# Windows of 320 and 512 slots, an earlier first read of the slots, and scatters that follow evictions one by one

## The chip, the cores and the metric

The kernel runs on one NeuronCore of a Trainium2 chip. The metric is the device time of one launch in microseconds. The core has TensorE (PE in the profile, with its weight loads in a row PEld of their own), VectorE (DVE), ScalarE (ACT), GpSimd (POOL) and SyncE (SP), which issues the plain DMAs; POOL issues the indirect ones. PSUM is where PE writes; DVE and ACT copy it out ("evict").

## The reference

A gated linear attention with a complex decay feeds a mixture of experts with top 2 of 8:

```python
# attention: q, k, v, a_re, a_im are (4, 8, 768, 48): batch, heads, time, dim
scale = np.minimum(mag, 0.999) / (mag + 1e-06)          # mag = |a|
for t in range(S):
    S_re, S_im = ar * S_re - ai * S_im + kv(t), ar * S_im + ai * S_re
    y[:, :, t] = einsum('bhd,bhde->bhe', q[:, :, t], S_re)
# experts: x is y as (3072, 384); 8 experts, 384 -> 1024 -> 384
noisy_logits = x @ w_gate + log1p(exp(x @ w_noise)) * noise
top2, top2_w = ...                                       # softmax over the two largest
for e in range(E):
    for k in range(2):
        mask = top2[:, k] == e
        h = np.maximum(x[mask] @ w1[e], 0.0)
        out[mask] += top2_w[mask, k, None] * (h @ w2[e])
```

## The kernel before

**Attention.** Time is cut into 6 chunks of 128 steps; a chunk of the 4 batch rows is a *group* g of 4 tiles, 24 tiles n in all (n = 4g + b). The decay is put in polar form: phase p1 and p2 work out log magnitude and angle for a pair of tiles, p2t sums the angles along time with a matmul by a triangle of ones. The last row of each tile's angles is carried into the same batch row's next tile: a small DMA stores it in `car`, and `p2carry` adds it. Before the change `car` is the first partition of the tile `xga`. Per tile, `tr_unit(n, 0)` and `tr_unit(n, 1)` transpose the turned q and k on PE, and ACT evicts them (L302: first qT, then kT); `sc_unit` makes the scores (L310), `st_unit` the state update (16 small matmuls into pG, at partitions 0 and 64 for real and imaginary part, L320), `y_unit` the output into pY (L357 from the state, L359 from the scores), which ACT copies into xT (L360). `x_unit` turns it back into rows of the tile `xr` (one per group, two buffers).

**Routing.** After each group `glog` and `gdis` work out the gates. `gate_dispatch` gives every token two slots in the DRAM tensor `xs`: expert e owns a region of its own, rows are handed out in order of arrival, and a row holds the token's 384 values, its 8 gate weights and its number. POOL writes them with indirect DMAs ("scatters", L421), 8 per group: 4 tiles times 2 choices, 128 rows of 1600 bytes each. Groups 4 and 5 are dispatched in two steps, of three tiles and one. Scatters of groups 0 to 2 with b > 0 also wait for the copy L360 (`YC`) of tile 4(g + 1) + b - 1.

**Experts.** Each expert takes up to CAP = 832 slots in two windows: window 0 holds slots 0 to 383, window 1 slots 384 to 831. `load_x(e, w, dst)` reads a window from `xs` into `xga` (window 0) or `xgb` (window 1); `x_T` transposes it and splits it in two rounded parts; `mm1` multiplies with w1 (L544: 8 blocks of 128 hidden units, 9 matmuls each: 3 slices of the inner dimension, times high by high, high by low, low by high), ACT and DVE evict with relu and split; `mm2` multiplies with w2 per tile of 128 slots (24 matmuls of 384 columns, L568), the seventh tile being a half one of 64 (16 matmuls, L573 and L576). The result is multiplied with the gate, added to rows of `out` that `gather_o` (L555) has fetched, and scattered back (L582).

**Order.** The order on every engine is fixed at build time: each piece is given a step (`at(step, f, ...)`, step n being about tile n), the pieces are written out in order of steps, and a scheduler places them by readiness, priority and its own estimates of durations. At run time an engine takes its instructions in that order, so one that waits holds all behind it. Experts 0 and 1 are woven into the attention's end: `load_x(0, 0, xga)` stands behind the scatters of group 3, `x_T(0, 0)` at step 19, `load_x(1, 0, xga)` right behind it, then `mm1(0, 0)`, and `x_T(1, 0)` at step 23.3. The scatters of one launch are declared free of each other in `xs`; a read of `xs` waits for all scatters written before it, and later scatters wait for that read. In `out` each scatter waits for the one before it. At the end counts are checked: if an expert has more than CAP or fewer than 640 tokens, or experts 0 or 1 have less than a window 0 of them when it is read, a flag sends the launch down a slow path that is not run with these inputs.

Of the kernel before, what the change touches and what calls it, by code (L numbers as in the profile page):

```python
# [9 lines left out]
F32 = mybir.dt.float32  # L10
# [5 lines left out]
OP = mybir.AluOpType  # L16
# [61 lines left out]
def kernel(  # L78
# [20 lines left out]
    FILL = 640  # L99
    NQ = 2  # L100
    RAW = 3
    WIN = ((0, 384), (384, CAP - 384))
    JS = ((0, 1, 2), (3, 4, 5, 6))

# [43 lines left out]
    nc.gpsimd.memset(none[:, RNO:RNO + 1], float(NONE))  # L150
    xga = cp.tile([128, 4, ROW], F32, name="xga")
    nc.gpsimd.memset(xga, 0.0)
    car = xga[0:1, :, 0:HD]
    ncnt = cp.tile([128, 2], F32, name="ncnt")
    zero = cp.tile([128, DM], F32, name="zero")
    nc.vector.memset(zero, 0.0)
    ones_f = cp.tile([128, 1], F32, name="ones_f")
    nc.vector.memset(ones_f, 1.0)
    bad = cp.tile([128, 2, NT], F32, name="bad")
# [81 lines left out]

    def p2carry(m):
        if m >= B // 2:
            th = T0[m][2][0:1]
            b = 2 * m % B
            nc.vector.scalar_tensor_tensor(th, car[:, b:b + 2], -2.0 * math.pi, th, op0=OP.mult, op1=OP.add)

    def p2t(n):
        b, g = bt(n)
        pt = psC.tile([128, 512], F32, name="cum")  # L250
        nc.tensor.matmul(pt[:, :HD], tri_t, T0[n // 2][2][:, b % 2, :], start=True, stop=True)
        if n % 2 == 0:
            TF[n // 2] = pf.tile([128, 2, 2, HD], F32, name="tf", bufs=2)
        tf = TF[n // 2][:, :, n % 2, :]
        if g:
            nc.scalar.activation(tf[:, 1, :], pt[:, :HD], AF.Identity, bias=b_rnd)
            nc.vector.scalar_tensor_tensor(tf[:, 0, :], tf[:, 1, :], -RND, pt[:, :HD], op0=OP.add, op1=OP.subtract)
        else:
            nc.vector.tensor_scalar(tf[:, 1, :], pt[:, :HD], RND, -RND, op0=OP.add, op1=OP.add)
            nc.vector.tensor_sub(tf[:, 0, :], tf[:, 1, :], pt[:, :HD])  # L260
        if g + 1 < NG:
            nc.sync.dma_start(car[:, b, :], tf[127:128, 0, :])

    def p2s(m):

# [29 lines left out]
    def tr_unit(n, i):  # L295
        x = (qh, kh)[i][n % NQ]
        store = (QT, KT)[i]
        store[n] = pa.tile([112, H, 128], F32, name=("qT", "kT")[i], bufs=2)
        p = psA.tile([128, H, 128], F32, name="ptr", bufs=1)[0:112]
        for h in range(H):  # L300
            nc.tensor.transpose(p[:, h, :], x[:, h, :, :].rearrange("p r x -> p (r x)")[:, 0:112], ident)  # L301
        nc.scalar.activation(store[n], p, AF.Copy)  # L302

    def sc_unit(n, half):
        if half == 0:
# [7 lines left out]
    def st_unit(n):  # L313
        b, g = bt(n)
        if g + 1 == NG:
            return
        x = kh[n % NQ]
        for r in range(2):
            for h in range(H):
                nc.tensor.matmul(pG[64 * r:64 * r + D, h, :], x[:, h, r, 0:D], V[n][:, h, :], start=True, stop=True)  # L320

    def st_upd(n):
# [20 lines left out]
    def y_unit(n):  # L343

        b, g = bt(n)
        if b == 0:
            XR[g] = pa.tile([128, B, ROW], F32, name="xr", bufs=2)
            nc.gpsimd.memset(XR[g][:, :, RNO + 1:ROW], 0.0)
            nc.gpsimd.tensor_copy(XR[g][:, :, RNO], tokid[:, g])
        XT[n] = pa.tile([128, H // 2, 128], F32, name="xT", bufs=6)  # L350
        for i in range(H // 2):
            for z in range(0 if g else 1, 2):
                for r in range(2):
                    h = 2 * i + r
                    o = pY[64 * r:64 * r + D, i, :]
                    if z == 0:
                        nc.tensor.matmul(o, Z[b][:, h, :], QT[n][:, h, :], start=True, stop=False, skip_group_check=True)  # L357
                    else:
                        nc.tensor.matmul(o, V[n][:, h, :], AM[n][:, h, :], start=not g, stop=True, skip_group_check=True)  # L359
        LAST['y'] = YC[n] = nc.scalar.activation(XT[n], pY, AF.Copy)  # L360
# [28 lines left out]
            nc.tensor.transpose(p[:, kk * 128:(kk + 1) * 128], xt[:, b, kk * 128:(kk + 1) * 128], ident)  # L389
        return p  # L390

    scat, behind, YC = [], [], {}

    def gate_dispatch(g, lo, hi, lz):
        n = hi - lo
# [13 lines left out]
        nc.vector.tensor_add(pos, p[:, :n * E].rearrange("p (b e) -> p b e", b=n),  # L409
                             base_run[:, None, :].to_broadcast([128, n, E]))  # L410
        nc.vector.tensor_add(base_run, base_run, p[:, n * E:(n + 1) * E])
        if g == NG - 3:
            nc.vector.tensor_copy(ncnt, base_run[:, 0:2])
        nc.vector.tensor_mul(oh, oh, pos[:, None].to_broadcast([128, 2, n, E]))
        sl = pa.tile([128, 2, n], U32, name=f"sl{n}", bufs=2)
# [3 lines left out]
        for b in range(n):  # L419
            for kk in range(2):  # L420
                d = nc.gpsimd.indirect_dma_start(  # L421
                    out=xs, out_offset=bass.IndirectOffsetOnAxis(ap=sl[:, kk, b:b + 1], axis=0),
                    in_=XR[g][:, lo + b, :], in_offset=None, bounds_check=E * N - 1, oob_is_err=False)
                for s in scat:
                    tc.declare_no_dep(d.ins, s.ins, reason="slots differ")
                scat.append(d)

                if g < NG - 3 and b:
                    behind.append((d, B * (g + 1) + b - 1))


    fill = {}
# [11 lines left out]


    x3 = xs.rearrange("(e i) r -> e i r", e=E)
    TW = [min(128, CAP - 128 * j) for j in range(7)]

    def load_x(e, w, dst):
        if w == 0:  # L450
            nc.sync.dma_start(dst[:, 0:3], x3[e, 0:384].rearrange("(p j) r -> p j r", j=3))
        else:
            nc.sync.dma_start(dst[:, 0:3], x3[e, 384:768].rearrange("(p j) r -> p j r", j=3))
            nc.sync.dma_start(dst[0:CAP - 768, 3], x3[e, 768:CAP])

    mctx = ctx.enter_context(ExitStack())
    mpools, psB = [], []  # L460
# [49 lines left out]
    def x_T(e, w):  # L510
# [11 lines left out]
        for kk in range(KD):  # L522
            x = XW[w, kk] = mt([128, 2, n], F32R, name=f"x{w}{kk}")
            p = ps_tile("px")
            for j in js:
                o = 128 * (j - js[0])
                gz = nc.tensor.transpose(p[:, o:o + TW[j]], src_t[0:TW[j], j - js[0], kk * 128:(kk + 1) * 128],  # L527
                                    ident[0:TW[j], 0:TW[j]])
                if (e, w) == (0, 1):
                    behind_of(gz, 'm')  # L530
# [21 lines left out]
    def gather_o(e):  # L552
        for j in range(7):
# [3 lines left out]
                in_offset=bass.IndirectOffsetOnAxis(ap=OX[e][0:w, j:j + 1], axis=0),  # L557
                bounds_check=N - 1, oob_is_err=False)

    def mm2(e, w):  # L560
        for j in (JS[0], JS[1] if e + 1 < E else (6, 3, 4, 5))[w]:
            n, o = TW[j], 128 * j - WIN[w][0]
            p = psO.tile([128, 512], F32, name="po")
            a, g = ao[j][0:n, :], GW[e][0:n, j:j + 1]
            if n == 128:
# [4 lines left out]
            else:  # L570
# [8 lines left out]
                nc.scalar.copy(lo, p[n:2 * n, :DM])  # L579
                nc.vector.scalar_tensor_tensor(a, lo, g, a, op0=OP.mult, op1=OP.add)  # L580
            nc.vector.scalar_tensor_tensor(a, p[0:n, :DM], g, a, op0=OP.mult, op1=OP.add)  # L581
            nc.gpsimd.indirect_dma_start(  # L582
                out=out, out_offset=bass.IndirectOffsetOnAxis(ap=OX[e][0:n, j:j + 1], axis=0),
                in_=a, in_offset=None, bounds_check=N - 1, oob_is_err=False)
# [34 lines left out]
    for g in range(NG):  # L619
        for lo, hi in ((0, B),) if g < NG - 2 else ((0, B - 1), (B - 1, B)):  # L620
            at(B * g + hi + .5 + P["gl"], glog, g, lo, hi)
            at(B * g + hi + .5 + P["gd"], gdis, g, lo, hi)
        if g == NG - 3:
            at(B * g + hi + .5 + P["gd"], load_x, 0, 0, xga)

    def consts2():
# [8 lines left out]

    def clear_out(i):
        nc.sync.dma_start(out[i * 256:(i + 1) * 256].rearrange("(n p) d -> p n d", p=128),
                          zero[:, None, :].to_broadcast([128, 2, DM]))

    at(-3, consts2)  # L640
    for i in range(N // 256):
# [25 lines left out]
            tc.add_manual_dep(first.ins, y.ins.name, after, reason="table")  # L667

    later = mybir.DependencyInfo(mybir.DependencyClass.Sync, mybir.DependencyReason.SCHED_ONLY)
    for d, n in behind:  # L670
        tc.add_manual_dep(d.ins, YC[n].ins.name, later, reason="pace")

    open_pool(ap)
    mp = mpools[-1]
# [231 lines left out]
```

## Time and profile before

| | |
|---|---|
| median of 3 runs | 768.4 us (766.48, 768.40, 770.28) |
| span of the profiled execution | 765.7 us |
| PE, PEld busy | 705.0 us (92%), 637.9 us (83%) |
| DVE, ACT, POOL busy | 414.5 us (54%), 336.3 us (44%), 176.5 us (23%) |
| moved by DMA | 100.17 MB, mean 131 GB/s |
| mean granted TensorE clock | 0.981 |

A span is from the first to the last instruction of the profiled execution; the runs' times are taken apart from it, and no time of its own is shown for that execution. Busy time of PE counts a matmul from its start to a modelled end, so overlapping matmuls are one stretch. In a timeline, each row is a start, a duration and a run of like instructions; behind it, in brackets, the engine's idle time before it and what ended it ("issue": nothing that the profile shows; "remote": a semaphore whose writer it cannot name).

### The profile page before, as it was taken

What the parts mean: (1) busy time and instruction counts of PE and PEld (TensorE: products, weight loads), DVE (VectorE), ACT (ScalarE), POOL (GpSimd) and SP (SyncE); (2) the same over time, 40 slices, a digit from 0 to 9 for tenths busy, and PEclk for the clock granted to TensorE, in tenths of its full rate; (3) what the DMA queues carried; (4) which work ended last, traced back from release to release, by engine and by line L of the source; (5) the groups of instructions that cost most, each with busy time, mean ns of one, the idle gap of its engine ahead of it and who ended that gap; (6) DMA issues with size and microseconds to landing.
All of it is one profiled execution on the core that took longest, in us unless ns stands there. A gap on an engine that the chain in (4) does not pass through costs nothing. (4 is left out here: it accounts for less than half of the span.)

```text
span 765.7 us, 13413 instructions
## 1 busy us (share of the span) xinstructions
PE 705.0 (92%) x5184; PEld 637.9 (83%) x5184; DVE 414.5 (54%) x936; ACT 336.3 (44%) x555; POOL 176.5 (23%) x187
## 2 busy tenths in 40 slices
PE   1689999989796798999999999999999999999995
PEld 0467687868585687999999999999999999999995
DVE  5779797959677546545426326426425425425321
ACT  6699989767574345134205205205304304313200
POOL 2000014120406131401423223223222312412312
PEclk9899999999998799999999999999999999999998
DMA  7567675632326352613525225225315314401200
GB/s 262 120 238 231 227 235 164 209 128 67 116 53 243 108 190 75 226 49 100 178 74 197 91 74 192 92 74 185 104 64 184 114 64 167 129 32 52 59 32 33
DMA packets 64089, 100.17 MB, mean 131 GB/s; under 512 B 26488, under 2 KB 46133, under 8 KB 64016
## 3 DMA queue, kind: packets, MB, share of 16 engines
q1 hardware_dynamic: 54464, 71.68, 29.9%
q0 software_dynamic: 9552, 27.54, 10.2%
q8 instruction: 43, 0.70, 0.4%
q14 instruction: 30, 0.25, 0.1%
HBM read 68.55 MB, written 32.08 MB: 131 GB/s over the span
## 5 line engine op out<-in xcount | busy, mean ns | idle before, releaser
L568 PE MATMUL po<-w2h,h 128*128 128x384 f32 x768 | 199.3, 336 | 0.0
L544 PE MATMUL ph<-x,w1h 128*128 128x448 f32 (+1 forms) x720 | 198.8, 355 | 0.0
L568 PEld LDWEIGHTS po<-w2h,h 128*128 128x128 f32 x768 | 138.5, 188 | 0.3
L544 PEld LDWEIGHTS ph<-x,w1h 128*128 128x128 f32 x720 | 132.3, 188 | 7.7
L568 PE MATMUL po<-w2l,h 128*128 128x384 f32 x384 | 128.3, 334 | 0.0
L582 POOL DMA_INDIRECT out_dram<-ao,ox x56 | 60.9, 1087 | 290.3 <-DVE ao L581 273.6
L544 PE MATMUL ph<-x,w1l 128*128 128x448 f32 (+1 forms) x360 | 126.7, 352 | 0.0
L549 DVE SCALAR_TENSOR_TENSOR h<-ph,h 128x384 fp32r<-128x384 f32 (+1 forms) x184 | 74.3, 437 | 91.3 <-ACT h L546 77.1
L546 ACT ACTIVATE h<-ph 128x448 fp32r<-128x448 f32 (+1 forms) x120 | 62.5, 521 | 127.1 <-PE ph L544 101.9
L581 DVE SCALAR_TENSOR_TENSOR ao<-po,gw,ao 128x384 f32<-128x384 f32 (+1 forms) x56 | 34.4, 614 | 145.3 <-PE po L568 142.3
L421 POOL DMA_INDIRECT xs<-xr,sl x48 | 56.6, 1180 | 240.7 <-DMA qk<-in_qk_dram 105.9
L568 PEld LDWEIGHTS po<-w2l,h 128*128 128x128 f32 x384 | 72.1, 188 | 0.1
L544 PEld LDWEIGHTS ph<-x,w1l 128*128 128x128 f32 x360 | 67.6, 188 | 3.4
L555 POOL DMA_INDIRECT ao<-out_dram,ox x49 | 52.5, 1071 | 42.9 <-DMA out_dram<-ao,ox 26.2
L489 ACT CAST w2h<-raw 128x768 fp32r<-128x768 f32 x32 | 25.2, 833 | 79.7 <-PE po L573 79.7
L531 ACT CAST x<-px 128x448 fp32r<-128x448 f32 (+1 forms) x42 | 20.9, 512 | 89.3 <-PE px L527 83.6
L310 PEld LDWEIGHTS psc<-qT,kT 112*128 112x128 f32 x384 | 49.9, 199 | 4.7 <-issue 1.6
L310 PE MATMUL psc<-qT,kT 112*128 112x128 f32 x384 | 53.4, 284 | 0.5 <-DVE h L549 0.4
L357 PE MATMUL pY<-qT,z 112*48 112x128 f32 x320 | 39.1, 278 | 7.9 <-issue 6.6
L359 PE MATMUL pY<-am,v 128*48 128x128 f32 x384 | 43.5, 276 | 2.0 <-DVE am L311 1.6
L311 DVE TENSOR_TENSOR am<-psc,mask 128x512 f32<-128x512 f32 x48 | 32.8, 686 | 13.8 <-PE psc L310 13.4
L301 PE MATMUL ptr<-ident,qh 128*112 128x128 f32 x192 | 28.2, 283 | 8.0 <-ACT kT L302 6.9
(210 smaller groups left out, 998.7 us busy)
## 6 DMA issues: line engine op xcount, KB each, us to landing
raw<-in_moe_w_dram SPq DMA_DIRECT2D x24, 512.0 KB
raw<-in_moe_w_dram SPq DMA_DIRECT2D x32, 384.0 KB
qk<-in_qk_dram SPq DMA_DIRECT2D x24, 384.0 KB
xga<-xs SPq DMA_DIRECT2D x8, 600.0 KB
xgb<-xs SPq DMA_DIRECT2D x8, 600.0 KB
re<-in_a_dram SPq DMA_DIRECT2D x12, 384.0 KB
im<-in_a_dram SPq DMA_DIRECT2D x12, 384.0 KB
v<-in_v_dram SPq DMA_DIRECT2D x24, 192.0 KB
```

The costliest lines, as they stand in the source:

```text
L310: nc.tensor.matmul(p[:, j, :], KT[n][:, h, :], QT[n][:, h, :], start=True, stop=True)
L311: LAST['am'] = nc.vector.tensor_mul(AM[n][:, 4 * half:4 * half + 4, :], p, mask[:, None, :].to_broadcast([128, 4, 128]))
L357: nc.tensor.matmul(o, Z[b][:, h, :], QT[n][:, h, :], start=True, stop=False, skip_group_check=True)
L359: nc.tensor.matmul(o, V[n][:, h, :], AM[n][:, h, :], start=not g, stop=True, skip_group_check=True)
L421: d = nc.gpsimd.indirect_dma_start(out=xs, out_offset=bass.IndirectOffsetOnAxis(ap=sl[:, kk, b:b + 1], axis=0), in_=XR[g][:, lo + b, :], i ...
L544: LAST['m'] = nc.tensor.matmul(p[:, :n], W1[e, kk][i][:, f * 128:(f + 1) * 128], XW[w, kk][:, j, :], start=(m == 0), stop=(m == len(ms) - 1))
L546: nc.scalar.activation(h[:, 0:n], p[:, :n], AF.Relu)
L549: LAST['h'] = nc.vector.scalar_tensor_tensor(h[:, dst:dst + b - a], p[:, a:b], 0.0, h[:, a:b].bitcast(F32), op0=OP.max, op1=OP.subtract)
L555: nc.gpsimd.indirect_dma_start(out=ao[j][0:w, :], out_offset=None, in_=out, in_offset=bass.IndirectOffsetOnAxis(ap=OX[e][0:w, j:j + 1], ax ...
L568: nc.tensor.matmul(p[:, :DM], HT[w, f][i][:, o:o + 128], W2[f // 2][k2][:, f % 2, :], start=(m == 0), stop=(m == len(ms) - 1))
L581: nc.vector.scalar_tensor_tensor(a, p[0:n, :DM], g, a, op0=OP.mult, op1=OP.add)
L582: nc.gpsimd.indirect_dma_start(out=out, out_offset=bass.IndirectOffsetOnAxis(ap=OX[e][0:n, j:j + 1], axis=0), in_=a, in_offset=None, bound ...
```

## The change

It has these parts:

- Windows of 320 and 512 slots. The half tile of 64 is now the third of window 0; window 1 is four full tiles, read by one DMA, window 0 by two. The last expert takes window 1's tiles in plain order.
- `load_x(0, 0, xga)` stands behind group 2 (G0 = 3 groups) and not group 3. The first count check is made there, against 320. The reads of window 0 go into a list EARLY, and scatters of groups 3 and later, as far as they are written after such a read, do not wait for it.
- `car` is a tile of its own with a partition for each batch row (32 b), and `p2carry` adds one row at a time. `zero` is dropped, and `none` takes its place.
- `xr` has three buffers.
- Pacing: a table PACE names for each scatter of groups 0 to 3 an ACT eviction that it must follow. For group g, with n0 = 4g + 8: nothing; kT of tile n0; the copy L360 of tile n0 - 1; qT and kT of n0 + 1; qT and kT of n0 + 2; qT of n0 + 3. Of group 4, the scatters of its second and third tile follow qT and kT of tiles 22 and 23.
- `st_unit` loops over heads outside and over the two halves inside.
- Scatters of one expert into `out` are declared free of each other.

```diff
-    WIN = ((0, 384), (384, CAP - 384))
+    G0 = 3
+    WIN = ((0, 320), (320, CAP - 320))
     JS = ((0, 1, 2), (3, 4, 5, 6))
+    TW = (128, 128, 64, 128, 128, 128, 128)
+    TO = (0, 128, 256, 0, 128, 256, 384)
...
-    car = xga[0:1, :, 0:HD]
+    car = cp.tile([128, HD], F32, name="car")
...
         if m >= B // 2:
-            th = T0[m][2][0:1]
-            b = 2 * m % B
-            nc.vector.scalar_tensor_tensor(th, car[:, b:b + 2], -2.0 * math.pi, th, op0=OP.mult, op1=OP.add)
+            for u in range(2):
+                th = T0[m][2][0:1, u, :]
+                p = 32 * (2 * m % B + u)
+                nc.vector.scalar_tensor_tensor(th, car[p:p + 1, :], -2.0 * math.pi, th, op0=OP.mult, op1=OP.add)
...
-            nc.sync.dma_start(car[:, b, :], tf[127:128, 0, :])
+            nc.sync.dma_start(car[32 * b:32 * b + 1, :], tf[127:128, 0, :])
...
-        for r in range(2):
-            for h in range(H):
+        for h in range(H):
+            for r in range(2):
                 nc.tensor.matmul(pG[64 * r:64 * r + D, h, :], x[:, h, r, 0:D], V[n][:, h, :], start=True, stop=True)
...
-            XR[g] = pa.tile([128, B, ROW], F32, name="xr", bufs=2)
+            XR[g] = pa.tile([128, B, ROW], F32, name="xr", bufs=3)
...
+    PACE = {}
+    for g in range(NG - 2):
+        n0 = B * g + 2 * B
+        later_on = [None, (EV, (n0, 1)), (YC, n0 - 1), (EV, (n0 + 1, 0)), (EV, (n0 + 1, 1)),
+                    (EV, (n0 + 2, 0)), (EV, (n0 + 2, 1)), (EV, (n0 + 3, 0))]
+        for i, ev in enumerate(later_on):
+            PACE[g, i // 2, i % 2] = (ev,) if ev else ()
+    for i, n in enumerate((NT - 2, NT - 1)):
+        for kk in range(2):
+            PACE[NG - 2, 1 + i, kk] = ((EV, (n, kk)),)
...
-                for s in scat:
+                for s in scat + (EARLY if g >= G0 else []):
                     tc.declare_no_dep(d.ins, s.ins, reason="slots differ")
                 scat.append(d)
-                if g < NG - 3 and b:
-                    behind.append((d, B * (g + 1) + b - 1))
+                for ev, n in PACE.get((g, b, kk), ()):
+                    behind.append((d, ev, n))
...
         if w == 0:
-            nc.sync.dma_start(dst[:, 0:3], x3[e, 0:384].rearrange("(p j) r -> p j r", j=3))
+            d = [nc.sync.dma_start(dst[:, 0:2], x3[e, 0:256].rearrange("(p j) r -> p j r", j=2)),
+                 nc.sync.dma_start(dst[0:64, 2], x3[e, 256:320])]
+            EARLY.extend(d)
         else:
-            nc.sync.dma_start(dst[:, 0:3], x3[e, 384:768].rearrange("(p j) r -> p j r", j=3))
-            nc.sync.dma_start(dst[0:CAP - 768, 3], x3[e, 768:CAP])
+            d = [nc.sync.dma_start(dst, x3[e, 320:CAP].rearrange("(p j) r -> p j r", j=4))]
...
-        for j in (JS[0], JS[1] if e + 1 < E else (6, 3, 4, 5))[w]:
+        for j in JS[w]:
...
-            nc.gpsimd.indirect_dma_start(
+            d = nc.gpsimd.indirect_dma_start(
                 out=out, out_offset=bass.IndirectOffsetOnAxis(ap=OX[e][0:n, j:j + 1], axis=0),
                 in_=a, in_offset=None, bounds_check=N - 1, oob_is_err=False)
+            for x in osc.setdefault(e, []):
+                tc.declare_no_dep(d.ins, x.ins, reason="tokens differ")
+            osc[e].append(d)
...
-        if g == NG - 3:
+        if g == G0 - 1:
             at(B * g + hi + .5 + P["gd"], load_x, 0, 0, xga)
...
-    for d, n in behind:
-        tc.add_manual_dep(d.ins, YC[n].ins.name, later, reason="pace")
+    for d, ev, n in behind:
+        tc.add_manual_dep(d.ins, ev[n].ins.name, later, reason="pace")
```

More of the change, by code (lines that the diff above doesn't have):

```diff
@@ L152 @@
     nc.gpsimd.memset(xga, 0.0)
-    car = xga[0:1, :, 0:HD]
+    car = cp.tile([128, HD], F32, name="car")
     ncnt = cp.tile([128, 2], F32, name="ncnt")
-    zero = cp.tile([128, DM], F32, name="zero")
-    nc.vector.memset(zero, 0.0)
     ones_f = cp.tile([128, 1], F32, name="ones_f")
@@ L301, in tr_unit @@
             nc.tensor.transpose(p[:, h, :], x[:, h, :, :].rearrange("p r x -> p (r x)")[:, 0:112], ident)
-        nc.scalar.activation(store[n], p, AF.Copy)
+        EV[n, i] = nc.scalar.activation(store[n], p, AF.Copy)
     def sc_unit(n, half):
@@ L390, in gate_tr @@
         return p
-    scat, behind, YC = [], [], {}
+    scat, behind, YC, EV, EARLY = [], [], {}, {}, []
+    PACE = {}
[8 more added lines that the diff above has]
+            PACE[NG - 2, 1 + i, kk] = ((EV, (n, kk)),)
     def gate_dispatch(g, lo, hi, lz):
@@ L446 @@
     x3 = xs.rearrange("(e i) r -> e i r", e=E)
-    TW = [min(128, CAP - 128 * j) for j in range(7)]
     def load_x(e, w, dst):
         if w == 0:
-            nc.sync.dma_start(dst[:, 0:3], x3[e, 0:384].rearrange("(p j) r -> p j r", j=3))
-        else:
-            nc.sync.dma_start(dst[:, 0:3], x3[e, 384:768].rearrange("(p j) r -> p j r", j=3))
-            nc.sync.dma_start(dst[0:CAP - 768, 3], x3[e, 768:CAP])
+            d = [nc.sync.dma_start(dst[:, 0:2], x3[e, 0:256].rearrange("(p j) r -> p j r", j=2)),
+                 nc.sync.dma_start(dst[0:64, 2], x3[e, 256:320])]
+            EARLY.extend(d)
+        else:
+            d = [nc.sync.dma_start(dst, x3[e, 320:CAP].rearrange("(p j) r -> p j r", j=4))]
+        return d
     mctx = ctx.enter_context(ExitStack())
@@ L525, in x_T @@
             for j in js:
-                o = 128 * (j - js[0])
+                o = TO[j]
                 gz = nc.tensor.transpose(p[:, o:o + TW[j]], src_t[0:TW[j], j - js[0], kk * 128:(kk + 1) * 128],
@@ L558, in gather_o @@
                 bounds_check=N - 1, oob_is_err=False)
+    osc = {}
     def mm2(e, w):
-        for j in (JS[0], JS[1] if e + 1 < E else (6, 3, 4, 5))[w]:
-            n, o = TW[j], 128 * j - WIN[w][0]
+        for j in JS[w]:
+            n, o = TW[j], TO[j]
             p = psO.tile([128, 512], F32, name="po")
@@ L622 @@
             at(B * g + hi + .5 + P["gd"], gdis, g, lo, hi)
-        if g == NG - 3:
+        if g == G0 - 1:
             at(B * g + hi + .5 + P["gd"], load_x, 0, 0, xga)
@@ L637, in clear_out @@
         nc.sync.dma_start(out[i * 256:(i + 1) * 256].rearrange("(n p) d -> p n d", p=128),
-                          zero[:, None, :].to_broadcast([128, 2, DM]))
+                          none[:, None, 0:DM].to_broadcast([128, 2, DM]))
     at(-3, consts2)
```

## The prediction

> **What bounds the kernel now.** I read the view by stages first, with borders set at the scatter bursts and at the one long hole, then the order of time around that hole. Columns of a stage row: its border, its length, busy time (and instructions) of PE, PEld, DVE, ACT, POOL, the granted TensorE clock, DMA share, GB/s.
>
> ```profile
> 111.80:126.00 14.20, 12.39 (x142) 10.44 (x139) 12.49 (x21) 13.50 (x19) 10.25 (x8) 1.00 0.73 263
> 126.00:149.10 23.10, 23.10 (x287) 19.79 (x283) 19.93 (x56) 18.04 (x33) 0.25 (x2) 1.00 0.51 140
> 149.10:161.00 11.90, 9.78 (x98) 7.31 (x96) 8.25 (x12) 5.99 (x8) 8.70 (x8) 0.94 0.67 228
> 161.00:191.90 30.90, 30.42 (x377) 26.70 (x376) 25.30 (x66) 26.09 (x44) 0.25 (x2) 0.97 0.30 83
> 191.90:205.00 13.10, 9.05 (x96) 6.96 (x95) 7.09 (x11) 6.63 (x8) 8.93 (x8) 1.00 0.43 156
> ...
> 265.70:279.00 13.30, 11.84 (x99) 10.55 (x97) 8.46 (x19) 7.42 (x12) 8.55 (x8) 1.00 0.75 238
> ```
>
> ```profile
> 242.40:253.40 11.00, 0.67 (x4) 0.24 (x4) 3.94 (x27) 1.02 (x3) 4.75 (x6) 0.62 0.41 150
> 253.40:259.20 5.80, 5.73 (x33) 4.74 (x33) 2.26 (x13) 1.21 (x3) 0.00 (x0) 0.55 0.28 104
> ...
> 302.40:757.50 455.10, 453.52 (x2517) 431.63 (x2515) 192.58 (x405) 125.72 (x221) 121.02 (x113) 1.00 0.33 110
> ```
>
> From 302 us on PE is busy for 453.5 of 455.1 us: the expert stage is PE's, and only less or shorter PE work makes it shorter. The attention stage before it is not one engine's. It has a hole of 11 us in which every compute engine stands, and stretches in which eight scatters (L421) leave POOL one behind the other. In those, PE is idle for 1.81, 2.12 and 4.05 us, in the stretches between for nothing and 0.48 us. The hole in order of time (start, duration, instruction, idle before it and what ended that):
>
> ```profile
> 242.12 0.28 PE L359 MATMUL pY<-am,v 128*48 128x128 f32 x1 [0.29 <-issue]
> 247.99 0.67 PE L357 MATMUL pY<-qT,z 112*48 112x128 f32 x4 [5.59 <-issue]
> 253.47 0.87 PE L527 MATMUL ptr<-ident,xga 128*128 128x128 f32 x3 [4.81 <-DMA xga<-xs]
> ```
>
> ```profile
> 246.77 1.06 POOL L421 DMA_INDIRECT xs<-xr,sl  x1 [0.30 <-issue]
> ...
> 247.34 0.60 ACT L360 ACTIVATE xT<-pY 128x512 f32<-128x512 f32 x1 [3.87 <-remote]
> ...
> 249.61 0.34 SPq L451 DMA_DIRECT2D xga<-xs  x1
> ...
> 253.36 0.17 DVE L517 COPY gw<-xga 128x3 f32<-128x3 f32 x1 [4.34 <-DMA xga<-xs]
> ```
>
> It has two halves. PE first waits 5.59 us for pY, which ACT's copy L360 frees only at 247.94; that copy waited 3.87 us for something the trace cannot name, inside group 3's burst. Then PE has come to the transposes of x_T(0,0) and waits 4.81 us for xga, whose load could start only when group 3's last scatter (issued at 246.77) had landed. After that the clock is 0.55 for 5.8 us.
>
> **The change, part by part.**
>
> *First load after three groups; car out of xga; windows of 320.* load_x(0,0) now follows group 2's scatters, and no carry row holds xga. Group 2's last scatter is paced behind the q eviction of tile 19; group 3's last one behind that of tile 23.
>
> ```profile
> 225.19 1.02 ACT L302 ACTIVATE qT<-ptr 112x1024 f32<-112x1024 f32 x1 [0.41 <-PE ptr L301]
> ...
> 287.45 1.02 ACT L302 ACTIVATE qT<-ptr 112x1024 f32<-112x1024 f32 x1 [0.44 <-PE ptr L301]
> ```
>
> ```profile
> 297.43 0.55 PE L527 MATMUL ptr<-ident,xga 128*128 128x128 f32 x3
> ```
>
> Counting back from tile 23 (287.45), tile 19's q eviction ends at 226.2. From a last scatter's start to the load's issue takes 249.61 - 246.77 = 2.84 us, the load 253.36 - 249.61 = 3.75 us, the issue behind an eviction some 0.3: 6.9 us in all. So xga is there at 233, nine us before PE asks. The load leaves the path: -4.8 us. The other half, 5.6 us, I also book, since at that place only single scatters are left: together -10.4. Without a hole there is no slow clock behind it: 5.8 x (1 - 0.55) = -2.6 us.
>
> What is late next is load_x(1,0), into the same xga. It is written after group 3's scatters, so it waits for all of them, and they now end behind tile 23's q eviction: 288.47 + 6.9 = 295.4, against 261.13 before. x_T(1,0) stands on PE at 297.43. That leaves 2 us; SP's weight loads, or a scatter of group 4 ahead of it on POOL (1.3 us each), use that up. Ends: 0, and +4 with three such scatters; I take +1. Group 5's scatters are unpaced and follow their gates as before. Their load xgb (issued at 315.78, below) feeds transposes at 329.41. The work in front shrinks by 8 x 176 ns in mm2(0,0), one tile being the half one, and 72 x 29 ns in mm1(1,0): 3.5 us less cover out of 329.41 - 315.78 - 3.75 = 9.9. Cost nothing.
>
> ```profile
> 315.78 0.40 SPq L453 DMA_DIRECT2D xgb<-xs  x1
> ```
>
> ```profile
> 329.41 1.37 PE L527 MATMUL px<-ident,xgb 128*128 128x128 f32 x8
> ```
>
> *Pacing.* The forty-eight scatters stay forty-eight POOL instructions of the same length; nothing is added but waits on ACT. Behind a waiting scatter on POOL stand only the next scatters and the small fills of xr, which no engine awaits soon, and xr with three buffers is free again before its next use. The gain is at most PE's idle time in the bursts of groups 0 to 2 and 4: 1.81 + 2.12 + 4.05 + 1.46 = 9.4 us. The other end is a loss: spaced scatters reach stretches that today are free of them, and half of the idle time might come again on top, +4. I take -6, nearer the gain, because the expert stage has 113 POOL instructions and PE idle for only 1.6 us. The Trainium skill, SBUF — State Buffer, "SBUF: two separate sides", speaks against this term: engine ports and DMA ports are disjoint, so a transfer does not slow an engine. By it the bursts only happen to coincide with PE's idle time, the term is nothing, and the sum is 755.
>
> *Columns of mm1.* Per expert 72 matmuls of 384 and 72 of 448 columns become 72 of 320 and 72 of 512.
>
> ```profile
> 411.58 0.34 PE L544 MATMUL ph<-x,w1l 128*128 128x384 f32 x1
> ...
> 421.06 0.34 PE L544 MATMUL ph<-x,w1l 128*128 128x384 f32 x1
> ```
>
> ```profile
> 422.70 0.37 PE L544 MATMUL ph<-x,w1l 128*128 128x448 f32 x1
> ...
> 427.04 0.37 PE L544 MATMUL ph<-x,w1l 128*128 128x448 f32 x1
> ```
>
> ```profile
> L544 PEld LDWEIGHTS ph<-x,w1h 128*128 128x128 f32 x720 | 132.3, 188 | 7.7
> ```
>
> ```profile
> 391.08 0.82 PE L527 MATMUL px<-ident,xga 128*128 128x128 f32 x6
> ```
>
> Every third matmul is a w1l: 9.48 us over 54 give 175.6 ns for 384 columns, 4.34 over 21 give 206.7 for 448, 0.457 and 0.461 ns a column. Pro rata 320 take 146 and 512 take 236: 382 a pair, as now. Zero, if a load of 128x128 weights fits into 146 ns. It lasts 188 but overlaps its neighbour; six loads with short matmuls behind them went every (0.82 - 0.28) / 5 = 109 ns. The evictions, transposes and the half tile (now in window 0) keep their number and total of columns.
>
> *st_unit by heads.* The halves 0 and 64 of pG now alternate.
>
> ```profile
> 238.12 1.36 PE L320 MATMUL pG<-v,kh 128*48 128x48 f32 x29
> ```
>
> ```profile
> 287.19 1.95 PE L310 MATMUL psc<-qT,kT 112*128 112x128 f32 x16
> ...
> 290.20 0.39 PE L359 MATMUL pY<-am,v 128*48 128x128 f32 x4
> ...
> 290.64 0.39 PE L359 MATMUL pY<-am,v 128*48 128x128 f32 x4
> ```
>
> Today one takes (1.36 - 0.21) / 28 = 41 ns. y_unit alternates the same halves: eight matmuls of 128 columns in 0.44 us, 55 ns each, where L310 with equal columns needs (1.95 - 0.28) / 15 = 111. Halved, 640 instructions save 13 us of PE; if the loads of 48 columns set the 41 ns, nothing. The Trainium skill, TensorE: Matmul & The Clock Gate, "The mechanism" under Part 3, says that a weight load overlaps running matmuls only where row groups differ; both halves use all rows, so by it the term is zero and the sum 750.4. Nearest is L320's own row, with 48 moving columns: I take a quarter, 3 us of PE, and half of that at the end, as PE is one of three busy engines there: -1.5.
>
> *Carry rows.* Ten additions of 1x768 become twenty of 1x384:
>
> ```profile
> L246 DVE SCALAR_TENSOR_TENSOR t<-xga,t 1x768 f32<-1x768 f32 x10 | 9.0, 940 | 0.1
> ...
> L257 DVE SCALAR_TENSOR_TENSOR tf<-tf,cum 128x384 f32<-128x384 f32 x20 | 10.8, 552 | 4.8 <-ACT tf L256 3.7 <-issue 0.7
> ```
>
> 20 x 552 - 10 x 940 = +1.6 us of DVE, on the path to p2t; +1. The dropped fill of zero lay in the start's load time: 0.
>
> *Scatters into out without order among themselves.* Usually POOL starts 0.28 us after DVE ends; the last scatter started 1.27 after.
>
> ```profile
> 738.10 0.62 DVE L581 SCALAR_TENSOR_TENSOR ao<-po,gw,ao 128x384 f32<-128x384 f32 x1 [3.54 <-PE po L568]
> 739.00 1.00 POOL L582 DMA_INDIRECT out_dram<-ao,ox  x1 [3.12 <-DVE ao L581]
> ...
> 757.52 0.62 DVE L581 SCALAR_TENSOR_TENSOR ao<-po,gw,ao 128x384 f32<-128x384 f32 x1 [3.54 <-PE po L568]
> 759.41 0.97 POOL L582 DMA_INDIRECT out_dram<-ao,ox  x1 [3.72 <-DMA out_dram<-ao,ox]
> ```
>
> -1.0 at the tail; elsewhere PE covers it. The last expert's new tile order ends on a full tile as before: 0.
>
> **Sum**, against this execution's span of 765.7: -10.4 - 2.6 + 1 - 6 + 0 - 1.5 + 1 - 1 = -19.5, a span of 746.2. The median of the runs, 768.4, lies 2.7 above this span; with that, 749.
>
> **Rivals.**
> 1. *Only the load goes.* The 5.59 us and the idle time of the bursts come from dependences, not from bunched scatters. For it: the releaser is unnamed, and the bursts fall where the angles of the next group are worked out. The page on SBUF is on its side. Against: three of three idle stretches coincide. Half of the slow clock stays: -4.8 - 1.3 + 1 - 1.5 + 1 - 1 = -6.6, so 762.
> 2. *More.* The bursts' idle time goes whole (3.4 more) and pG's halves overlap fully (13 x 0.5 - 1.5 = 5 more): 741.
> 3. *x_T(1,0) late by 6 to 8 us*, with a slow clock behind it, when SP puts weight loads ahead of load_x(1,0): 756.
> 4. *Slower: weight loads set the pace of the 320s.* No row of mm1 shows a load and matmul pair below 176 ns. At 176 the 576 matmuls of 320 cost 576 x 30 ns = +17: 766, no change. From 146 + (19.4 + 3.8) / 0.576 = 186 ns it is slower, and the load's 188 gives 24 us more: 773. Against: the 109 ns above.
>
> **How the numbers follow.** Chances: my sum 0.50 (own range 744 to 756), rival 1 0.20, rival 2 0.13, rival 3 0.05, rival 4 0.12, more of it on the slow side. Half a per cent, 3.8 us, is about what runs of this kernel can tell. Faster: 0.50 + 0.13 + 0.05 and most of rival 1, 0.84; same, the rest of rival 1 and part of rival 4, 0.09; slower 0.07. From 741 to 764 holds half of rival 2, the sum, and rivals 1 and 3: 0.8.
>
> **What would show it.** Right: no PE idle time over 2 us between 200 and 290, the clock near 1.00 there, xga issued at least 8 us before its first transpose; scatters singly, and PE idle under 1 us in any 12 us of attention; 320 columns at about 146 ns and 512 at 236; L320 below 41; the last scatter 0.3 us behind DVE. Wrong: PE waiting for xga before x_T(1,0), an idle ACT ended by "remote" with no burst near it, or 320 columns at 170 ns or more.

## The result, and the profile after

The changed kernel takes 737.85 us (median of four runs, 736.88 to 740.60) beside 769.34 for the kernel before (766.48 to 771.58): a ratio of 0.961, 95% interval 0.957 to 0.964. That is faster, as forecast, but by 31 us where the forecast had 19, and 3 us below its range.

The profiled execution has a span of 738.9 us (own time 740.60) against 765.7. Its view by stages, columns as above:

```profile
111.30:126.00 14.70, 14.45 (x152) 11.54 (x147) 12.64 (x22) 13.79 (x20) 6.81 (x5) 1.00 0.74 259
126.00:145.00 19.00, 18.67 (x258) 15.59 (x257) 17.67 (x51) 16.99 (x31) 3.79 (x5) 1.00 0.58 160
145.00:176.50 31.50, 30.98 (x410) 25.74 (x409) 29.89 (x69) 29.61 (x48) 8.71 (x10) 1.00 0.51 150
176.50:212.00 35.50, 33.89 (x414) 27.05 (x411) 31.22 (x85) 27.25 (x45) 10.19 (x10) 1.00 0.35 99
212.00:240.00 28.00, 25.87 (x290) 21.76 (x290) 21.01 (x68) 12.44 (x23) 8.88 (x9) 0.94 0.53 185
240.00:277.30 37.30, 33.80 (x340) 29.58 (x338) 20.66 (x81) 19.64 (x37) 10.38 (x11) 1.00 0.46 152
277.30:731.30 454.00, 452.50 (x2515) 418.14 (x2514) 191.45 (x397) 126.12 (x220) 115.31 (x113) 1.00 0.34 111
731.30:738.90 7.60, 0.00 (x0) 0.00 (x0) 0.62 (x1) 0.00 (x0) 0.97 (x1) 0.81 0.08 26
```

The expert stage went from 455.1 to 454.0 us, the tail from 8.2 to 7.6, the start by half a microsecond. All the rest, 190.6 to 166.0, came out of the attention stage between the first scatters and the first output matmul. POOL's work now lies in every row of it instead of in bursts of eight scatters, and there is no stage in which PE stands for most of the time. The order of time around the old hole (start, duration, instruction, idle before it and what ended that):

```profile
216.29 0.33 SPq L462 DMA_DIRECT2D xga<-xs  x1
216.67 0.49 SPq L463 DMA_DIRECT2D xga<-xs  x1
```

```profile
226.19 0.64 PE L537 MATMUL ptr<-ident,xga 128*128 128x128 f32 x3 [2.06 <-ACT kT L304]
```

The load is issued 9.9 us before PE needs it, and what PE waits for there is an eviction of ACT. The second load into the same tile, the forecast's "late next":

```profile
264.60 0.33 SPq L462 DMA_DIRECT2D xga<-xs  x1
...
269.37 0.17 DVE L527 COPY gw<-xga 128x3 f32<-128x3 f32 x1 [2.31 <-DMA xga<-xs]
...
271.85 0.64 PE L537 MATMUL ptr<-ident,xga 128*128 128x128 f32 x3
```

It is there 2.5 us before its transposes, and PE does not wait. A matmul of st_unit (L322, before L320) takes (0.93 - 0.21) / 31 = 23 ns where it took 41, and the 48-column work of the whole run falls from 31.62 us of PE (before) to 20.09 (after); these are the rows of the two kernels' st_unit line alone (PE and PEld):

```profile
206.63 0.93 PE L322 MATMUL pG<-v,kh 128*48 128x48 f32 x32
```

```profile
0.00:765.00 765.00, 31.62 (x640) 28.46 (x640) 0.98 0.41 131
```

```profile
0.00:738.90 738.90, 20.09 (x640) 17.09 (x640) 0.99 0.43 136
```

mm1's 320 columns go every 0.44 / 3 = 147 ns, its 512 columns every 4.20 / 18 = 233 ns (every third matmul is a w1l), 380 a pair against 382:

```profile
394.73 0.31 PE L554 MATMUL ph<-x,w1l 128*128 128x320 f32 x1
395.17 0.31 PE L554 MATMUL ph<-x,w1l 128*128 128x320 f32 x1
...
396.91 0.40 PE L554 MATMUL ph<-x,w1l 128*128 128x512 f32 x1
...
401.11 0.40 PE L554 MATMUL ph<-x,w1l 128*128 128x512 f32 x1
```

576 pairs at 2 ns are the 1.1 us of the expert stage. The tail's last scatter starts 0.28 us after DVE ends:

```profile
731.30 0.62 DVE L593 SCALAR_TENSOR_TENSOR ao<-po,gw,ao 128x384 f32<-128x384 f32 x1 [3.54 <-PE po L580]
732.20 0.97 POOL L594 DMA_INDIRECT out_dram<-ao,ox  x1 [3.19 <-DVE ao L593]
```

### The profile page after: what moved, and what is told of

The parts are those of the page before. It is cut to its first block, busy times and chain, and to the rows that moved or that the text cites. A ratio compares the mean times of both kernels' runs of the same rounds, so it can differ in the third digit from the quotient of the medians.

```text
span 738.9 us, 13414 instructions
## 1 busy us (share of the span) xinstructions
PE 691.6 (94%) x5184; PEld 611.6 (83%) x5184; DVE 414.3 (56%) x945; ACT 336.6 (46%) x555; POOL 171.2 (23%) x187
## 4 chain that ended last, share of the span: by engine, by line
PE 65%; DVE 4%; ACT 3%; issue 3%; DMA 3%; SPq 0%; POOL 0%; POOLq 0%; DVEq 0%; ACTq 0%
PE ph L554 28%; PE po L580 27%; PE px L537 3%; PE po L585 2%; PE po L588 2%; DMA raw<-in_moe_w_dram 1%; ACT tr L201 1%; PE psc L312 1%; PE ptr L303 1%; PE pY L361 1%; DMA xs<-xr,sl 1%; DMA xga<-xs 1%; PE pY L359 1%; DVE qk L285 0%; DVE am L313 0%
## 5 line engine op out<-in xcount | busy, mean ns | idle before, releaser
L554 PE MATMUL ph<-x,w1h 128*128 128x512 f32 (+1 forms) x720 | 194.6, 354 | 0.2 <-ACT x L541 0.2
L554 PEld LDWEIGHTS ph<-x,w1h 128*128 128x128 f32 x720 | 127.9, 188 | 16.2 <-ACT x L541 0.7
L554 PE MATMUL ph<-x,w1l 128*128 128x512 f32 (+1 forms) x360 | 127.6, 355 | 0.0
L559 DVE SCALAR_TENSOR_TENSOR h<-ph,h 128x512 fp32r<-128x512 f32 (+2 forms) x176 | 73.2, 453 | 88.9 <-ACT h L556 73.0
L594 POOL DMA_INDIRECT out_dram<-ao,ox x56 | 54.7, 977 | 285.5 <-DVE ao L593 279.6
L556 ACT ACTIVATE h<-ph 128x512 fp32r<-128x512 f32 (+1 forms) x120 | 61.2, 522 | 117.6 <-PE ph L554 85.0
L433 POOL DMA_INDIRECT xs<-xr,sl x48 | 53.8, 1120 | 216.6 <-DMA qk<-in_qk_dram 104.5
L500 DVE TENSOR_TENSOR w2l<-raw,w2h 128x768 fp32r<-128x768 f32 x32 | 30.7, 959 | 13.6 <-ACT w2h L499 12.1
L359 PE MATMUL pY<-qT,z 112*48 112x128 f32 x320 | 37.4, 279 | 0.0
L591 ACT COPY lo<-po 64x384 f32<-64x384 f32 x8 | 3.8, 477 | 73.4 <-PE po L588 73.3
```

The source lines that it names most:

```text
L433: d = nc.gpsimd.indirect_dma_start(out=xs, out_offset=bass.IndirectOffsetOnAxis(ap=sl[:, kk, b:b + 1], axis=0), in_=XR[g][:, lo + b, :], i ...
L554: LAST['m'] = nc.tensor.matmul(p[:, :n], W1[e, kk][i][:, f * 128:(f + 1) * 128], XW[w, kk][:, j, :], start=(m == 0), stop=(m == len(ms) - 1))
L556: nc.scalar.activation(h[:, 0:n], p[:, :n], AF.Relu)
L559: LAST['h'] = nc.vector.scalar_tensor_tensor(h[:, dst:dst + b - a], p[:, a:b], 0.0, h[:, a:b].bitcast(F32), op0=OP.max, op1=OP.subtract)
L594: d = nc.gpsimd.indirect_dma_start(out=out, out_offset=bass.IndirectOffsetOnAxis(ap=OX[e][0:n, j:j + 1], axis=0), in_=a, in_offset=None, b ...
```

## The experiments

The theory I went in with: a run of eight scatters holds up the signals between the engines, and spacing them gives that time back, more than PE's idle time in the bursts had shown. The rivals: the waits do nothing and the third buffer of xr does it ("rival D" below); the gain is that of the earlier load alone; the order of st_unit carries more than was booked. All variants are made from the changed kernel, except where the text says "the kernel before". Kernels named together ran in one session, each beside the kernel before.

**First session: one part undone at a time.** The kernel before took 763.12 us here.

a_nopace:

```diff
+    PACE = {}
```

> The changed kernel without any pacing (PACE emptied): scatters leave POOL as soon as their slots are known; early read, third buffer of xr and all else stay. Theory S (eight scatters in a row hold the other engines up, and spacing them takes that away): the idle stretches return, PE idle 1.5 to 4 us in each of the bursts of groups 0 to 3, time 744 to 749. Rival D (the idle stretches came from dependences that the third buffer and the new order removed): no change, 736 to 740.

a_nopace_xr2, the same with

```diff
-            XR[g] = pa.tile([128, B, ROW], F32, name="xr", bufs=3)
+            XR[g] = pa.tile([128, B, ROW], F32, name="xr", bufs=2)
```

> The changed kernel without pacing and with two buffers of xr instead of three. Theory S: as without pacing alone, within 2 us, since the buffer was only needed because paced scatters hold xr longer. Rival D: the missing buffer brings the idle stretches back, 6 us or more over the kernel that only lacks pacing.

a_st_old:

```diff
-        for h in range(H):
-            for r in range(2):
+        for r in range(2):
+            for h in range(H):
```

> The changed kernel with the old loop order in st_unit (all heads of one half, then of the other). The prediction's term: +1.5 us, about 739.5. Rival (the halves overlap fully, 41 ns down to some 24, and PE is what the attention stage waits for): 11 us of PE come back and half or more of it reaches the end, 743 to 748. If PE's time there were slack: 736 to 739.

a_late4, the first load after group 3 again, with group 3's scatters unpaced, because the load would otherwise wait for tile 23:

```diff
-    G0 = 3
+    G0 = 4
...
-    for g in range(NG - 2):
+    for g in range(NG - 3):
```

> The changed kernel with the first read of window 0 behind group 3 again (G0 = 4) and group 3's scatters unpaced; groups 0 to 2 stay paced. The hole in front of x_T(0,0) should return. By the prediction's two terms (both halves of the hole and the slow clock) +13 us: 750 to 752. Rival (the 5.6 us half of the hole and part of the slow clock belonged to something else that the change removed, only the wait for xga returns): 742 to 745. If the scheduler finds other work for PE meanwhile: under 741.

| kernel | us (runs) | ratio to before, 95% |
|---|---|---|
| a_nopace | 756.75 (752.72 to 762.06) | 0.993 (0.990 to 0.996) |
| a_nopace_xr2 | 759.74 (753.24 to 764.12) | 0.995 (0.991 to 0.999) |
| a_st_old | 742.38 (741.48 to 743.21) | 0.976 (0.973 to 0.979) |
| a_late4 | 744.79 (743.54 to 746.84) | 0.979 (0.975 to 0.982) |

The changed kernel itself did not run beside these. It took 737 to 738 us in each of the three in which it did, with the kernel before at 769, 754 and 754 us, and the costs that follow are measured against that, across sessions. The pacing is worth most: without it three quarters of the gain are gone, more than theory S expected (744 to 749). The third buffer alone can't be told from nothing: without it the kernel takes 3 us more, half of rival D's 6, and the two kernels' runs overlap. Undoing the loop order costs some 5 us. Undoing the earlier load (with group 3's burst back) costs some 7, which is the rival's 742 to 745 and not the 13 of the prediction's two terms.

Where a_nopace loses, its stages show: the bursts of groups 1 and 2 and the stretches before, between and behind them.

```profile
123.00:150.00 27.00, 25.47 (x335) 21.05 (x336) 23.55 (x63) 24.42 (x41) 0.81 (x2) 1.00 0.51 142
150.00:161.00 11.00, 8.92 (x77) 6.73 (x72) 8.20 (x16) 7.32 (x11) 8.62 (x8) 0.99 0.65 206
161.00:189.00 28.00, 27.59 (x355) 23.02 (x354) 25.64 (x67) 23.61 (x41) 0.63 (x3) 0.94 0.28 70
189.00:199.50 10.50, 5.91 (x76) 4.31 (x76) 4.47 (x8) 3.52 (x6) 8.05 (x8) 0.95 0.59 224
199.50:228.60 29.10, 27.69 (x298) 21.97 (x298) 23.16 (x71) 21.90 (x37) 1.18 (x3) 0.90 0.35 93
```

In the bursts PE issues 7 instructions in a microsecond, before and between them 12 to 13. From the end of the first of these bursts on the granted clock is below 1: 0.94, 0.95 and 0.90 in the last three rows. In order of time in the second of these bursts, ACT, DVE and PE pass work on by signals:

```profile
191.52 1.56 PE L253 MATMUL cum<-t,tri_t 128*128 128x384 f32 x4
...
197.94 0.58 ACT L258 ACTIVATE tf<-cum,b_rnd 128x384 f32<-128x384 f32 x1 [6.17 <-remote]
198.48 0.97 POOL L434 DMA_INDIRECT xs<-xr,sl  x1 [0.30 <-issue]
198.55 0.55 DVE L259 SCALAR_TENSOR_TENSOR tf<-tf,cum 128x384 f32<-128x384 f32 x1 [5.05 <-issue]
...
199.16 1.65 PE L253 MATMUL cum<-t,tri_t 128*128 128x384 f32 x2 [4.39 <-DVE tf L259]
```

L258 reads the product that PE started at 191.52. It starts 6.4 us later, released by something that the trace cannot name ("remote"). Behind it DVE starts after standing for 5.05 us, and PE after 4.39. PE had worked on behind that product up to 194.77, so it is the handing on that is late, or ACT's taking it up. POOL meanwhile goes on.

**Second session: more scatters, and the tail.** Here the kernel before took 754.42 us. after_again is the changed kernel. a_extra400 adds eight scatters of 1600-byte rows to each of groups 0 to 3, unpaced, into a tensor of their own; a_extra16 the same with rows of 64 bytes. Their results are not used.

```diff
+            for kk in range(2):
+                d = nc.gpsimd.indirect_dma_start(
+                    out=xdum, out_offset=...sl[:, kk, b:b + 1]..., in_=XR[g][:, lo + b, 0:400], ...)
```

> The changed kernel once more, so that the others of this call have it beside them on the same chip. About 738 to 741; the kernel without pacing was 14.5 us longer in its profiled execution (753.4 against 738.9), and the medians of different calls can differ by some us.

> The changed kernel, and for each of groups 0 to 3 eight more scatters of 128 rows of 1600 bytes into a DRAM tensor that nothing reads, unpaced, one behind the other as soon as the slots are known; the real scatters stay paced. PE, DVE and ACT have the same instructions in the same order. Theory Q (the bytes of a burst, 1.6 MB a group, are what holds the others up): 12 to 20 us over the changed kernel. Theory G (the making of indirect transfers by POOL in a row, whatever their bytes): the same 12 to 20 us. If bursts do no harm by themselves: under 3 us.

> As the kernel with eight more unpaced scatters per group, but each row is 64 bytes and not 1600: same number of transfers and rows, a twenty-fifth of the bytes. Theory Q: under 3 us over the changed kernel. Theory G: within 4 us of the one with 1600 bytes, so 8 to 20 us over.

a_osc_old puts back the order among the scatters into out:

```diff
-            for x in osc.setdefault(e, []):
-                tc.declare_no_dep(d.ins, x.ins, reason="tokens differ")
-            osc[e].append(d)
```

> The changed kernel with the scatters into out again waiting for one another. Prediction's term: +1.0 us, all at the tail (the last scatter 1.3 us behind DVE and not 0.3). The profile after shows 0.6 us of that.

Measured: after_again 737.23 us (ratio 0.976, 0.974 to 0.979), a_extra400 735.90 (0.975, 0.973 to 0.976), a_extra16 735.53 (0.975, 0.974 to 0.977), a_osc_old 736.56 (0.976, 0.974 to 0.979). Here, with the kernel before at 754, up to fourteen scatters in a row cost nothing, where theories Q and G had 12 to 20 us for a_extra400; whether they would cost something where the kernel before takes 763 was not run. The declaration at the tail can't be measured here, and with the old order declared the last scatter starts just as soon:

```profile
728.42 0.62 DVE L593 SCALAR_TENSOR_TENSOR ao<-po,gw,ao 128x384 f32<-128x384 f32 x1 [3.54 <-PE po L580]
729.31 0.97 POOL L594 DMA_INDIRECT out_dram<-ao,ox  x1 [3.19 <-DVE ao L593]
```

The last expert's new order of tiles is not what moved the last scatter either. The kernel b_w320 of the fourth session has that order and the old declaration, and there the last scatter starts 1.26 us after DVE ends, behind the scatter before it. The two kernels ran in different sessions, so what the declaration is worth where the kernel before takes 763 stays open.

**Third session: chip, target, or scatters at all?** New was the question why the kernel before had taken 769, 763 and 754 us in three sessions, and the changed one 737 to 738 in the two that had it. after_c3 is the changed kernel, a_nopace2 and a_extra400b repeat the kernels of those names. a_dupxs scatters the rows of groups 0 to 3 into xs twice, unpaced first:

```diff
+                d = nc.gpsimd.indirect_dma_start(
+                    out=xs, ..., in_=XR[g][:, lo + b, :], ...)
+                for s in dups + scat + (EARLY if g >= G0 else []):
+                    tc.declare_no_dep(d.ins, s.ins, reason="slots differ")
+                dups.append(d)
```

> The changed kernel itself, beside the next three on one chip. Both theories: 734 to 741 us, as on the three chips before it. The kernel before took 769, 763 and 754 us on those; by the theory that runs of scatters cost time only on some chips, the next run's result goes with what the kernel before takes here.

> All waits behind evictions taken out again, as in a_nopace (756.75 us where the kernel before took 763). Theory 1, runs of eight scatters hold up signals between engines, more on some chips than on others: if the kernel before takes 760 to 770 here, 752 to 762; if it takes 754, 738 to 746. Theory 2, the waits themselves change the order of the work: 752 to 760 on every chip.

> Eight more unpaced scatters of 1600-byte rows per group 0 to 3, into a tensor of their own. Theory 1 with the chip as the cause: 745 to 755 where the kernel before takes 760 to 770, 734 to 738 where it takes 754. Theory 3, only scatters into xs do harm (its rows lie 768 apart by expert and many land near each other): 734 to 738 on every chip.

> The same eight rows per group 0 to 3 are scattered into xs twice, first unpaced, then as in the changed kernel. Theory 1: as a_extra400b in this call. Theory 3: 745 to 755 on every chip, at least 6 us over a_extra400b.

| kernel (before: 753.90) | us (runs) | ratio to before, 95% |
|---|---|---|
| after_c3 | 738.36 (736.38 to 740.38) | 0.979 (0.977 to 0.982) |
| a_nopace2 | 735.88 (733.23 to 737.48) | 0.974 (0.971 to 0.978) |
| a_extra400b | 735.69 (734.02 to 736.80) | 0.974 (0.972 to 0.977) |
| a_dupxs | 737.98 (736.70 to 739.77) | 0.978 (0.975 to 0.981) |

The kernel that took 756.75 us takes 735.88, if anything a little less than the paced one. The waits as such do not make the kernel faster (theory 2), and theory 1 is right only as long as it says "not always". Theory 3 fails as it stands, "on every chip"; but as unpaced scatters into xs cost nothing at this time, whether the target matters where they do cost was not tested. The same burst as above, stage and order of time, in a_nopace2:

```profile
180.00:190.50 10.50, 10.50 (x113) 8.25 (x113) 9.80 (x18) 9.77 (x15) 7.24 (x7) 1.00 0.65 231
```

```profile
183.32 1.56 PE L253 MATMUL cum<-t,tri_t 128*128 128x384 f32 x4
184.02 0.97 POOL L434 DMA_INDIRECT xs<-xr,sl  x1 [0.30 <-ACT qT L304]
184.28 1.23 ACT L258 ACTIVATE tf<-cum,b_rnd 128x384 f32<-128x384 f32 x2 [0.34 <-PE cum L253]
...
185.57 1.01 DVE L259 SCALAR_TENSOR_TENSOR tf<-tf,cum 128x384 f32<-128x384 f32 x2
...
186.26 0.94 PEld L253 LDWEIGHTS cum<-t,tri_t 128*128 128x128 f32 x4 [0.18 <-DVE tf L259]
```

POOL sends off its scatters just as densely and the DMA moves as much (231 GB/s against 224). But ACT starts 0.96 us behind PE's start instead of 6.4, and PE issues 113 instructions instead of 76. It is one program, on the same data, so the two profiled executions show where its stalls cost time. Their spans are 753.4 us (a_nopace) and 734.8 (a_nopace2). PE is idle for 56.2 and 46.9 us of them and busy for 697.2 and 687.9: half of the loss shows as idle time, half as busy time. Some 5 us of the second half are the clock. PE works through the last three rows of a_nopace above at 0.94, 0.95 and 0.90; the rows' lengths times what is missing from 1 give an estimate of 1.7 + 0.5 + 2.9 us, while a_nopace2 has a clock of 1.00 from 109.5 to 275 us.

**Fourth session: the other parts, by themselves.** Before: 763.41 us, on the chip of the third session. b_copy is the kernel before, a_st_old2 and a_late4b repeat the kernels of the first session, b_w320 is the kernel before with the windows of 320 and 512 alone:

```diff
-    WIN = ((0, 384), (384, CAP - 384))
+    WIN = ((0, 320), (320, CAP - 320))
```

(with TW, TO, load_x and mm2's order as in the change).

> The kernel before itself, for its profile on another chip. Theory 1, runs of eight scatters stall the engines on some chips only: where it takes about 754 us, no PE idle time over 2 us in the scatter runs before 205 us and x_T(0,0) 10 us or more earlier than the 253.5 of the first profile, with what is left of the hole the wait for xga alone (4 to 6 us). Theory 2, the hole and the idle time are the kernel's own and the chip is slower elsewhere: the hole of 11 us stands here too.

> The changed kernel with st_unit's old order of loops, 640 matmuls at 42 ns instead of 23.6, 11 us of PE. If half of it lies on the path: 742 to 744 us. If other engines cover it: 737 to 740 us.

> The changed kernel with the first load after group 3 again and group 3's scatters unpaced. Theory 1 where the kernel before takes 754: the load costs what PE waits for it, 4 to 6 us, so 741 to 745. If the hole came from the stalled scatters alone: 736 to 739. Where the kernel before takes 760 to 770: 744 to 748, as on the chip before.

> The kernel before with windows of 320 and 512 alone. By the step times of the profile after (147 + 229 ns a pair against 175.6 + 206.7) 576 pairs give 3.6 us less: a ratio of 0.995. If the expert stage hides it, as its 453.9 us against 455.1 say: 0.998 to 1.000.

Measured: b_copy 763.10 us (0.999, 0.998 to 1.001), a_st_old2 743.32 (0.974, 0.972 to 0.976), a_late4b 744.57 (0.975, 0.973 to 0.977), b_w320 761.87 (0.999, 0.997 to 1.001). So the kernel before took 753.90 and 763.41 on one chip at two times: the chip is not what decides. b_copy could not answer its question for 754 us, as it took 763; at that time its profile has the hole again, PE waiting 5.50 and then 4.86 us in front of x_T(0,0). The loop order is worth 5 us and the load 7, as in the first session; the windows by themselves give nothing that can be measured, which agrees with 2 ns a pair. What the later load costs is one wait of PE:

```profile
228.50 0.34 SPq L462 DMA_DIRECT2D xga<-xs  x1
...
231.79 0.96 PE L537 MATMUL ptr<-ident,xga 128*128 128x128 f32 x3 [7.24 <-DMA xga<-xs]
```

**Fifth session.** Before: 763.58 us, on the same chip. b_copy2 is the kernel before again, b_st_new the kernel before with st_unit's loops by heads (the diff of a_st_old backwards).

> The kernel before once more. One chip gave 753.9 us for it at one time and 763.4 at another, so its time does not go with the chip. If it takes about 754 here: PE's idle time in the scatter runs before 205 us falls from 8 us to under 2, and what stands in front of x_T(0,0) is a wait for xga of 4 to 6 us. If about 763: the same hole as in the two profiles so far, 10 to 11 us between pY of tile 19 and x_T(0,0).

> The kernel before with st_unit's loops by heads alone. Half of its 11 us of PE on the path: ratio 0.992 to 0.994 (5 us). Covered by other engines there: 0.998 to 1.001. The forecast's quarter, half exposed: 0.998.

b_copy2 took 762.60 us (0.999, 0.997 to 1.001), so again no profile of the kernel before at 754 us came of it; the hole is there, with waits of 7.42 and 2.95 us. b_st_new took 768.57 (1.006, 1.004 to 1.009): slower, which neither the theory nor a rival expected. It saves the same 11 us of PE and loses more in the bursts. Group 1's burst, first in b_copy2, then in b_st_new:

```profile
148.00:161.00 13.00, 12.49 (x127) 10.54 (x127) 11.23 (x19) 11.05 (x17) 9.26 (x8) 1.00 0.76 253
```

```profile
150.00:163.00 13.00, 7.07 (x39) 4.54 (x40) 5.46 (x9) 5.03 (x8) 6.66 (x8) 0.93 0.46 165
```

PE gets 39 instructions done in 13 us instead of 127. In one execution each, such a stall strikes one burst and spares another, but over twelve runs the kernel with the shorter PE work was the slower one. Its clock was lower as well: 0.968 to 0.979 in its runs, lower in the slower ones, and 0.979 to 0.986 in those of the kernel before. On 768 us the difference of the means, 0.974 and 0.982, is an estimated 6 us of PE work. The same edit that is worth 5 us on spaced scatters (across sessions) costs 5 on bunched ones, at a time when the kernel before takes 763. Why the bursts stall b_st_new more isn't shown.

## Why the prediction was right and wrong

Right: the direction, the place (the attention stage), and most of the signs that it named: the load 9.9 us ahead, no wait for it, x_T(1,0) on time, 320 and 512 columns at 147 and 233 ns (forecast 146 and 236), the scatters mostly singly, the last scatter 0.28 us behind DVE. Three signs did not come. PE's longest wait near the old hole is 2.06 us (forecast: none over 2), the clock is 0.94 from 212 to 240 (forecast: near 1.00), and from 240 to 277.3 PE is idle for 3.5 us (forecast: under 1 in any 12). Rival 4 (weight loads set the pace of the 320s) and rival 3 (x_T(1,0) late) did not happen. Rival 2, "more", came nearest with 741 us: its overlap in pG held, and its other reason, the bursts' idle time, was only part of what the bursts cost.

Wrong: the size, in three terms of the sum. Between the two profiled executions PE's idle time fell by 13.4 us (60.7 to 47.3) and its busy time by as much (705.0 to 691.6). The prediction had 16.4 of its 19.5 us in idle time.

- *Pacing, -6 with bounds of -9.4 and +4.* It was worth about 19 us where the kernel before takes 763 (756.75 without, 737 to 738 with, across sessions; 14.5 between the two profiled executions, 753.4 and 738.9), and nothing, or 2.5 us the other way, where it takes 754. The first lies far outside the bounds, and that there are two values was not in them at all. Two steps failed. First, PE's idle time in the bursts was taken as the most that could come back. Between those two executions idle time makes 8.9 of the 14.5 us (56.2 to 47.3), near the bound; the other 5.6 is PE's busy time (697.2 to 691.6), which the term put at nothing. The prediction booked a slow clock behind the hole alone, but one follows the bursts as well: 0.94, 0.95 and 0.90 in a_nopace's rows, an estimated 5 us, and 0.94 and 0.97 stood in the prediction's own rows at 149.10 and 161.00. Second, one profile was taken for the kernel's price, though it is the price of a session. The Trainium skill, SBUF — State Buffer, "SBUF: two separate sides", had spoken against this term. Where the kernel before takes 754 us the runs agree with it; where it takes 763 the rows of L258 show ACT starting late behind PE at an unchanged DMA rate, and what holds it is not shown.
- *The hole, -10.4 - 2.6.* The later load costs 7 us (a_late4, a_late4b, with group 3's burst in it), more than the 4.8 booked for it: PE comes to x_T(0,0) sooner and waits 7.24 us in a_late4b, where the changed kernel waits 2.06, and the clock is 0.86 from 228.5 to 260 behind it. The first half (ACT's copy held by something "remote" for 3.87 us inside a burst) has the signs of the stall shown in a_nopace, and then belonged into the term above. That is argued, not shown: in a_late4b, whose group 3 burst is unpaced, it does not stand apart from the wait for xga.
- *st_unit, -1.5.* 640 instructions went from 41 to 23 ns, 11.5 us of PE, and undoing it costs 5 (742.38 and 743.32 us): the quarter should have been nearly the whole, the half exposed was right. The row of y_unit, which the prediction had quoted, was the better guide (55 ns with alternating halves against 111) than L320's own. The Trainium skill, TensorE: Matmul & The Clock Gate, "The mechanism" under Part 3, lets a weight load overlap only where row groups differ; both halves use all 128 rows, and the trace shows the overlap all the same, as a load that lasts 124 ns goes every 23. The measurement decides.

The parts undone one by one make 19 + 7 + 5 = 31 us where the kernel before takes 763, while the changed kernel's 737 to 738 us, from other sessions, is only 25 to 26 below 763. They overlap, and b_st_new shows how far: with bunched scatters the loop order has the opposite sign. Where the kernel before takes 754 the change gives 16 to 17; load and loop order would make 12 of it if they cost there what they cost elsewhere. That wasn't measured there, and 4 us have no name.

Carry rows (+1), the tail (-1) and the windows (0) are too small for these runs. Of the 11.1 us by which the forecast missed the median, the span accounts for 7.3 (738.9 for 746.2). The other 3.8 are the offset: the profiled execution was the longest of its four, so the median lies 1.05 below its span and not 2.7 above.

What stays open is why one program takes 754 us at one time and 763 to 769 at another. One thing goes with it in every trace: where the kernel before takes 754, a trace holds some 8,740 semaphore updates (8,735 to 8,741 in after_again, after_c3 and a_nopace2; over 9,100 in the four runs with more scatters), elsewhere 7,177 to 7,519 (before, after, a_nopace, a_st_old, b_copy and b_w320), with almost the same instructions. The records that are missing are missing from the trace, not from the program. "Remote" goes with them: it ends waits in eleven of the twelve traces that hold fewer updates and in none of the eight others, so it may be no more than the mark of a missing record, and names no cause. Whether recording itself delays the signals when scatters come in a row, or something else delays both, no run here separates; every run was recorded.

## What to carry to other kernels

Where bursts of DMA stand beside unexplained waits, add to the idle time what the granted clock loses in the stages behind it: here the loss was half idle time, half busy time. And repeat the kernel before at another time, because the price of a burst may belong to the session. Spacing the scatters is then insurance more than speed: it cost 2.5 us at most in one session and saved some 19 in another (compared across sessions), and the changed kernel took the same time (737 to 738 us) in each of the three sessions in which it ran. The loop order was worth 5 us with the stalls gone and cost 5 with them there, so the order of such edits matters.

## What the runs showed of the hardware

- In a run of eight scatters, the ACT instruction that reads a product of PE (L253 to L258) started 6.4 us after PE's start in one session and 1.0 us in another, in one program and at nearly equal DMA rates (224 and 231 GB/s).
- Behind such stalls the granted TensorE clock was 0.94, 0.95 and 0.90 in three stages, where the same program without them had 1.00.
- Matmuls whose weights have 48 columns and whose outputs lie in alternating halves of the partitions, with all 128 rows in use, went every 23 ns instead of 41.
- fp32r matmuls of 320 and 512 columns went every 147 and 233 ns beside 128x128 weight loads of 188 ns: the load did not set the pace.
